# Recurrence and soft mixture of experts on one core: ScalarE evicts y ahead of VectorE, and the bonus products, the outer products, the row exponentials and one r*k product change their places in the written order

## The chip, the cores and the metric

The kernel runs on one core of a Trainium2 chip. Its engines are TensorE (PE, with its weight loads PEld), VectorE (DVE), ScalarE (ACT), GpSimd (POOL) and SyncE (SP), which issues all the DMAs. The metric is the device time of one execution in microseconds (us).

## The reference

Two parts follow each other. The first is a recurrence over 768 steps with a decaying state, for 4 batches of 8 heads of 48 channels:

```python
for t in range(S):                      # S = 768, B = 4, H = 8, D = 48
    cur = einsum('bhd,bhe->bhde', u[None] * kt, vt)          # the bonus u
    y[:, :, t] = einsum('bhd,bhde->bhe', rt, state + cur)
    state = wt[:, :, :, None] * state + einsum('bhd,bhe->bhde', kt, vt)
```

The second takes y as x (3072 rows of 384) through a soft mixture of 8 experts with 4 slots each:

```python
logits = x @ phi                                     # 3072 x 32
d = softmax over the rows;   slot_input = d.T @ x    # 32 x 384
slot_out[e] = relu(slot_input[e] @ w1[e]) @ w2[e]    # 384 -> 1024 -> 384
c = softmax over the 32 columns;   out = c @ slot_out
```

## The kernel before

**Staging.** A loop `for n in range(NIT + 1)` (L711, NIT = 16) makes one pair of heads in each iteration; `b, j = divmod(n, 4)` are its batch and its place in the batch. The 768 steps are cut into 6 chunks of 128. In what follows, "j=2" is an iteration with that j. After the loop (L839 on) come the last softmax over the rows, the experts (`up_proj`, `up_relu`, `turn`, `down_proj`) and the mixing of their outputs (`mix`).

**Order.** Nothing is scheduled by a planner: `tc.manual_schedule()` (L434) leaves every engine its instructions in the order in which they are written, and only the semaphores between the engines are put in for it, from the tiles that are read and written. So the order of the lines in the loop is the order of each engine's queue.

**The steps of iteration n** (m = n - 1 and l = n - 2 are earlier pairs whose later steps run in the same iteration), with the engine and the line under which the profile lists them:

- `b_pat(n)`: ACT L541. `b_kn(n)`: five transposes of k on PE (L548), four of them into the PSUM bank `tp1` and the fifth into `kn4`, a part of the bank `tp0`; then two copies on ACT, L550 out of `tp1` and L552 out of `kn4`.
- `c_inter(m)` (PE L615, 40 matmuls) and `c_av(m)` (PE L624, 48 matmuls) make y of the pair before in two banks `yb[0]`, `yb[1]` of one PSUM tile `y`; `c_evac(m)` adds the bonus term `avs` and writes `x`: DVE L635 for the first head, ACT L637 (a copy) and POOL L638 (the addition) for the second.
- `b_u(n)`: the outer products of k and v into `U`, in the bank `tp0` (PE L581). `b_state(n)`: a scan over them (DVE L590, `Traw`). `b_tc(n)`: ACT L597.
- `b_scores(n, hf)`: scores of one half of the chunks into the two banks of `ap` (PE L559, 12 matmuls). `b_at(n, hf)`: their eviction (ACT L564) and mask (POOL L566). Both halves use the same banks, so the second scores wait for the first eviction.
- `b_bonus(n)`: 24 small matmuls of r*k with u into `aP`, in the bank `tp0` too (PE L573), for j < 3 alone. `b_a(n)`: their copy (ACT L587). `b_av(n)`: POOL L602/L604 and L606.
- The preparation of later units u of r, k and the decays w: `a_rk` (POOL L512, r*k), `a_back` (DVE L517 scan, L520; POOL L521), `a_k` (DVE L525), `a_fwd` (DVE L528 scan), `a_r` (DVE L534), `a_chk` (POOL L537). `a_k(u)` overwrites the k that `a_rk(u)` reads.
- The softmaxes of the batch before: `l_turn(l, ypp)` turns finished x through the two banks of `y` (PE L73, ACT L650) at the end of an iteration; `l_mm` (PE L77), `s_max` (DVE L87, L88), `s_turns` (PE L109, L111; ACT L113, L115), `s_mm` (PE L120) lie between the two halves of the scores. `s_rows_exp` (DVE L145, POOL L146, ACT L147) ends the iterations with j=0 of b=2 and b=3, `s_norm` (DVE L151 to L153, POOL L154) those with j=1.

`keep_warm` (PE L674) issues matmuls on zeros. In the tail, `up_relu` evicts one half of the experts' hidden values, 512 columns, in two parts, DVE L203 and ACT L204.

Of the kernel before, what the change touches and what calls it, by code (L numbers as in the profile page):

```python
# [22 lines left out]
C = S // P  # L23
# [26 lines left out]
def rwkv_soft_moe(ctx: ExitStack, tc: tile.TileContext, wc, krc, vc, cst, w1, w2, out):  # L50
# [91 lines left out]
    def s_rows_exp(q, eng=nc.vector):  # L142
        ce = q["ce"]
        q["rm"] = rm = small.tile([P, 2 * NTG, 1], F32, name="rm")
        nc.vector.tensor_reduce(out=rm, in_=ce, axis=AX.X, op=ALU.max)  # L145
        eng.tensor_tensor(out=ce, in0=ce, in1=rm.broadcast_to([P, 2 * NTG, NS]), op=ALU.subtract)  # L146
        nc.scalar.activation(out=ce, in_=ce, func=AF.Exp)  # L147

    def s_norm(b, q, eng=nc.vector):
        ce, rm = q["ce"], q["rm"]  # L150
# [49 lines left out]

    def up_relu(h_sb, hp, hf):
        lo = 512 * hf
        nc.vector.tensor_scalar(h_sb[:, lo:lo + 256], hp[:, 0:256], 0.0, None, op0=ALU.max)  # L203
        nc.scalar.activation(out=h_sb[:, lo + 256:lo + 512], in_=hp[:, 256:512], func=AF.Relu)  # L204

    def turn(h_sb, hT, f4, tps):
        for n in range(2):
# [299 lines left out]
    def a_rk(u, k=None, c0=0, cn_=C):  # L507
        t = kr4[u % 4]
        k = t[:, 0:ROW] if k is None else k
        k3 = k.rearrange("p (c e) -> p c e", e=PIT)[:, c0:c0 + cn_, 1:PIT]  # L510
        r3 = t[:, RO:KRW].rearrange("p (c e) -> p c e", e=PIT)[:, c0:c0 + cn_, 0:P]
        nc.gpsimd.tensor_tensor(out=rks[u % 2][:, c0:c0 + cn_], in0=k3, in1=r3, op=ALU.mult)  # L512
# [31 lines left out]
    def b_kn(n):  # L544
        kt = Kt(n)
        for c in range(C - 1):
            o = tp[1][:, c * PITCH:(c + 1) * PITCH] if c < 4 else kn4
            nc.tensor.transpose(out=o, in_=kt[0:PITCH, c * PIT + 1:c * PIT + PIT], identity=ident[0:PITCH, 0:PITCH])  # L548
        src = bass.AP(tensor=tp[1].tensor, offset=tp[1].offset, ap=[tp[1].ap[0], [64, 2], [PITCH, 4], [1, D]])
        nc.scalar.copy(out=kns[n % 2][:, :, 0:4], in_=src)  # L550
        src = bass.AP(tensor=kn4.tensor, offset=kn4.offset, ap=[kn4.ap[0], [64, 2], [1, D]])
        nc.scalar.copy(out=kns[n % 2][:, :, 4], in_=src)  # L552
# [10 lines left out]
    def b_at(n, hf):  # L563
        nc.scalar.copy(out=ats[n % 2][hf].rearrange("p h c t -> p h (c t)"), in_=app[:, :, 0:384])  # L564
        at = ats[n % 2][hf].rearrange("p h c t -> p (h c) t")
        nc.gpsimd.affine_select(out=at, in_=at, pattern=[[0, 6], [1, P]], compare_op=ALU.is_gt,  # L566
                                fill=0.0, base=0, channel_multiplier=-1)

    def b_bonus(n):
        b, g = divmod(n, NG)  # L570
        for c in range(C if g < NU else 0):
            for p in range(0, P, 64):
                nc.tensor.matmul(out=aP[p:p + 64, c, :], lhsT=rks[(NU * b + g) % 2][:, c, p:p + 64],  # L573
                                 rhs=ub[:, g, :], start=True, stop=True)

    def b_u(n):
        kn, vt = kns[n % 2], vts[n % 3]
        first = [True, True]
        for c in range(C - 1):
            for h in range(2):  # L580
                nc.tensor.matmul(out=U[64 * h:64 * h + D, :, c + 1], lhsT=kn[:, h, c, :], rhs=vt[:, c, h, :],  # L581
                                 start=first[h], stop=(c == C - 2))
                first[h] = False

    def b_a(n):
        if n % NG < NU:
            nc.scalar.copy(out=asb[n % 2], in_=aP)  # L587

    def b_state(n):
        nc.vector.tensor_tensor_scan(  # L590
            out=Traw[0:PITCH].rearrange("p e n -> p (e n)"),
            data0=U[0:PITCH].rearrange("p e n -> p (e n)"),
            data1=pats[n % 2][0:PITCH].rearrange("p e n -> p (e n)"),
            initial=0.0, op0=ALU.add, op1=ALU.mult)
# [33 lines left out]
    def c_evac(n, last=False):  # L628
        b, g = divmod(n, NG)
        x = xb[b % 2]  # L630
        for h in range(2):
            xh = x[:, :, (2 * g + h) * D:(2 * g + h + 1) * D]
            yh = yb[h][:, 0:C * D].rearrange("p (c d) -> p c d", d=D)
            if h == 0 or last:
                nc.vector.tensor_tensor(out=xh, in0=yh, in1=avs[n % 2][:, h], op=ALU.add)  # L635
            else:
                nc.scalar.copy(out=xh, in_=yh)  # L637
                nc.gpsimd.tensor_tensor(out=xh, in0=xh, in1=avs[n % 2][:, h], op=ALU.add)  # L638

    def l_turn(n, pp, split=False):  # L640
        b, g = divmod(n, NG)
# [69 lines left out]
    for n in range(NIT + 1):  # L711
        b, j = divmod(n, NG)
        live = n < NIT
        m, l = n - 1, n - 2
        lb, lj = divmod(l, NG)
        sb_ = b - 1
        soft = live and 0 <= sb_ < B - 1

        u_next = NU * (b + 1) + j - 1
        if n == 0:  # L720
            a_load_w(2)
            a_load_kr(2)
        if j == 1 and live:
            a_gather(NU * b)
        if j in (1, 2) and live:
            a_gather(NU * b + j)
        if j >= 1 and u_next < B * NU and live:
            a_load_w(u_next)
            a_load_kr(u_next)
        if n + 1 < NIT:  # L730
            v_load(n + 1)
        if live:
            for _ in range(PIECES[n]):
                weight_piece()

        u0 = NU * b
        nxt = b + 1 < B
        if live:
            b_pat(n)
            if n == 0:  # L740
                a_rk(1)
                a_back(1)
            elif j == 0:
                a_fwd(u0 + 1)
                a_r(u0 + 1)
                a_chk(u0 + 1)
            elif j == 1:
                a_k(u0 + 2)
                a_fwd(u0 + 2)
            elif j == 2 and nxt:  # L750
                a_back(u0 + 3)
            elif j == 3 and nxt:
                a_r(u0 + 3)
                a_chk(u0 + 3)
                a_back(u0 + 4)
        if n == NIT:
            q = qs[b - 2]
            sp0 = tp[0][0:TG, 0:DM]
            s_mm(xb[b % 2], q, sp0)
            l_turn(l, app)  # L760
            l_mm(0, xTs[0], lpv, True, False)
            s_acc(b - 2, q, sp0)
            s_sum(b - 2, q)
            s_rows_exp(q)
            s_norm(b - 2, q)

        if live:
            b_kn(n)
        if m >= 0:
            c_inter(m)  # L770
            c_av(m)
            c_evac(m, n == NIT)
        if live:
            b_u(n)
            if n == 0:
                keep_warm(4, ap[0])
            b_scores(n, 0)
            b_at(n, 0)
            b_state(n)
        if j == 0 and b > 1 and live:  # L780
            q = qs[b - 2]
            s_mm(xb[b % 2], q, spv)
            s_acc(b - 2, q, spv)
            s_sum(b - 2, q)
        if soft and j == 1:
            l_mm(0, xTs[0], lpv, True, False)
            l_mm(1, xTs[1], lpv, False, True)
            nc.scalar.copy(out=lt_t, in_=lpv)
        if soft and j == 2:
            l_mm(2, xTs[0], lpv, True, True)  # L790
            nc.vector.tensor_tensor(out=lt_t, in0=lt_t, in1=lpv, op=ALU.add)
            qs[sb_] = q = s_max(sb_, lt_t)
        if soft and j == 3:
            s_turns(qs[sb_], dpv, lnv)
        if live:
            b_bonus(n)

        if live:
            if n == 0:
                a_k(1)  # L800
                a_fwd(1)
                a_r(1)
                a_chk(1)
            if j == 0:
                a_rk(u0 + 2)
                a_back(u0 + 2)
            elif j == 1:
                if nxt:
                    a_rk(u0 + 3)
                a_r(u0 + 2)  # L810
                a_chk(u0 + 2)
            elif j == 2 and nxt:
                a_k(u0 + 3)
                a_fwd(u0 + 3)
            elif j == 3 and nxt:
                a_rk(u0 + 4)
                a_k(u0 + 4)
        if live:
            b_a(n)
            b_tc(n)  # L820
            b_av(n)
        if live:
            if n == 0:
                keep_warm(4, ap[0])
            b_scores(n, 1)
            b_at(n, 1)
            if n == 0:
                keep_warm(8, yb[0])
        if l >= 0 and lj >= 1 and live:
            l_turn(l, ypp)  # L830
        if soft and j == 2:
            s_exp(sb_, q)
        if j == 0 and 1 < b and live:
            s_rows_exp(qs[b - 2], nc.gpsimd)
        if j == 1 and 1 < b:
            s_norm(b - 2, qs[b - 2], nc.gpsimd)


# [179 lines left out]
```

## Time and profile before

| what | value |
|---|---|
| time of the kernel, median of 3 runs (lowest to highest) | 215.06 us (213.92 to 216.74) |
| the profiled execution: its own time, its span | 215.24 us, 213.5 us |
| busy: PE, PEld, DVE, ACT, POOL | 178.5, 135.5, 111.6, 84.5, 88.1 us |
| chain that ended last: PE, DVE, POOL, ACT, DMA, issue | 54%, 14%, 10%, 7%, 6%, 5% of the span |
| mean granted TensorE clock over the span | 0.92 |
| ACT x L637 waiting for DVE x L635 | 36.6 us in 13 waits |

How to read it: the profile is one execution. The timeline gives start and duration in us from the start of the span, engine, line, operation, tiles (out<-in), shapes and the count of merged instructions; a bracket tells the idle time of the engine ahead of it and what ended that. "Windows" give, for a stretch of time, each engine's busy time with the count of its instructions in brackets, then the granted clock of TensorE (1.00 is full speed), the share of the DMA engines and GB/s. "Waits" give total us, times and the longest.

### The profile page before, as it was taken

To read this page: it belongs to the slowest core of one execution; us is meant where nothing else is said; L and a number is where in the kernel's file an instruction comes from. 1 tells how busy PE (TensorE), PEld (TensorE's weight loads), DVE (VectorE), ACT (ScalarE), POOL (GpSimd) and SP (SyncE) were. 2 spreads that over 40 slices of the span, in tenths; PEclk is the share of its full clock that TensorE was granted. 3 is DMA by queue.
4 is the path that set the end of the run, shared out by engine and by line. 5 is a ranking of instruction groups with operands and counts; after the bars stand their busy time and mean duration, and the time that the engine had idled before them with its cause. 6 is when DMAs were issued, how large, how long until landed. Compare 5 with 4: busy or idle time off the path is not lost.

```text
span 213.5 us, 7814 instructions
## 1 busy us (share of the span) xinstructions
PE 178.5 (84%) x3397; PEld 135.5 (63%) x3400; DVE 111.6 (52%) x183; ACT 84.5 (40%) x187; POOL 88.1 (41%) x130
## 2 busy tenths in 40 slices
PE   7887699977899987998988888998997977898840
PEld 2455589866797876776867766887643223776630
DVE  5886752949534594697485886142433231015330
ACT  3323051672508447355566454666512111103230
POOL 4343473685617539384665584664600000000000
PEclk9999655999559996999999999999999999999995
DMA  5995568399956849996949982699486099005682
GB/s 156 379 315 115 225 154 360 104 390 290 308 201 183 331 113 329 354 312 205 328 167 359 394 202 109 150 410 413 154 300 276 11 358 392 8 3 205 259 356 86
DMA packets 15065, 52.11 MB, mean 244 GB/s; under 512 B 1968, under 2 KB 2736, under 8 KB 15024
## 3 DMA queue, kind: packets, MB, share of 16 engines
q1 hardware_dynamic: 15024, 51.55, 69.2%
q8 instruction: 28, 0.46, 0.9%
q14 instruction: 13, 0.11, 0.1%
HBM read 44.44 MB, written 4.72 MB: 230 GB/s over the span
## 4 chain that ended last, share of the span: by engine, by line
PE 54%; DVE 14%; POOL 10%; ACT 7%; DMA 6%; issue 5%; SPq 1%; ACTq 0%; DVEq 0%; POOLq 0%
PE ap L559 10%; PE y L624 9%; DMA krb<-in_krc_dram 6%; PE G L196 5%; PE y L232 5%; DVE G L517 4%; PE y L615 4%; PE tp L581 3%; PE tp L77 3%; POOL blkat L566 3%; POOL av L606 3%; POOL blka L512 3%; PE tp L573 3%; ACT blkat L564 2%; DVE G L528 2%
## 5 line engine op out<-in xcount | busy, mean ns | idle before, releaser
L624 PE MATMUL y<-v,blkat 128*64 128x48 f32 x768 | 30.0, 238 | 4.1 <-POOL blkat L566 3.7
L564 ACT COPY blkat<-ap 128x768 f32<-128x768 f32 x32 | 25.6, 800 | 19.0 <-PE ap L559 17.7
L566 POOL TENSOR_SCALAR_AFFINE_SELECT blkat<-blkat 128x768 f32<-128x768 f32 x32 | 27.6, 863 | 8.3 <-ACT blkat L564 8.2
L624 PEld LDWEIGHTS y<-v,blkat 128*64 128x64 f32 x768 | 27.2, 151 | 5.7 <-POOL blkat L566 4.2
L559 PE MATMUL ap<-krb 48*128 48x128 f32 x288 | 25.8, 315 | 1.1 <-issue 1.0
L638 POOL TENSOR_TENSOR x<-x,av 128x288 f32<-128x288 f32 x15 | 12.0, 801 | 29.7 <-ACT x L637 29.7
L635 DVE TENSOR_TENSOR x<-y,av 128x288 f32<-128x288 f32 x17 | 7.7, 456 | 29.9 <-PE y L624 29.9
L559 PEld LDWEIGHTS ap<-krb 48*128 48x128 f32 x288 | 20.7, 210 | 3.1 <-issue 2.0
L517 DVE TENSOR_TENSOR_SCAN G<-blkw,G 128x774 f32<-128x774 f32 (+1 forms) x13 | 21.4, 1643 | 1.6 <-DMA blkw<-in_wc_dram 1.3
L528 DVE TENSOR_TENSOR_SCAN G<-blkw,G 128x774 f32<-128x774 f32 (+1 forms) x13 | 21.5, 1650 | 0.5
L637 ACT COPY x<-y 128x288 f32<-128x288 f32 x15 | 6.0, 400 | 36.6 <-DVE x L635 36.6
L512 POOL TENSOR_TENSOR blka<-krb 128x768 f32<-128x768 f32 x11 | 17.1, 1553 | 4.0 <-DMA krb<-in_krc_dram 3.2
L525 DVE TENSOR_TENSOR krb<-krb,G 128x774 f32<-128x774 f32 (+1 forms) x13 | 11.6, 891 | 12.6 <-POOL blka L512 12.6
L573 PEld LDWEIGHTS tp<-cst,blka 128*64 128x64 f32 x288 | 10.2, 145 | 6.8 <-issue 5.0
L606 POOL TENSOR_TENSOR av<-v,asb 128x576 f32<-128x576 f32 x12 | 14.1, 1177 | 0.0
L590 DVE TENSOR_TENSOR_SCAN Traw<-tp,blkm 112x288 f32<-112x288 f32 x16 | 12.0, 751 | 3.3 <-PE tp L581 3.3
L581 PE MATMUL tp<-v,blkm 128*48 128x48 f32 x320 | 11.2, 222 | 2.6 <-ACT blkm L552 2.6
L573 PE MATMUL tp<-cst,blka 128*64 128x4 f32 x288 | 11.2, 205 | 2.4 <-DVE Traw L590 1.4
L232 PE MATMUL y<-wa,x 128*32 128x160 f32 (+1 forms) x144 | 12.2, 275 | 0.7 <-issue 0.7
L615 PE MATMUL y<-Tc,krb 48*64 48x48 f32 x480 | 10.6, 236 | 2.4 <-ACT blkm L650 2.4
L196 PE MATMUL G<-wa,siT 128*32 128x512 f32 x96 | 11.3, 597 | 1.4 <-ACT x L204 1.1
L615 PEld LDWEIGHTS y<-Tc,krb 48*64 48x64 f32 x480 | 9.1, 148 | 4.8 <-ACT blkm L650 3.8
(152 smaller groups left out, 328.6 us busy)
## 6 DMA issues: line engine op xcount, KB each, us to landing
wa<-in_w_dram SPq DMA_DIRECT2D x24, 512.0 KB, 7.9
krb<-in_krc_dram SPq DMA_DIRECT2D x11, 774.5 KB, 6.4
v<-in_vc_dram SPq DMA_DIRECT2D x16, 288.0 KB, 6.1
blkw<-in_wc_dram SPq DMA_DIRECT2D x11, 387.0 KB, 3.6
wa<-in_w_dram SPq DMA_DIRECT2D x6, 640.0 KB, 5.6
out_dram<-wa SPq DMA_DIRECT2D x4, 960.0 KB, 4.4
krb<-in_w_dram SPq DMA_DIRECT2D x4, 640.0 KB, 8.4
blka<-krb SPq DMA_DIRECT2D x24, 96.8 KB, 4.7
```

What stands on the lines that cost most here:

```text
L196: nc.tensor.matmul(out=hp[32 * g:32 * g + NS, :], lhsT=siT[:, e * KT + kt, :], rhs=wts[e][:, kt * F + hf * 512:kt * F + hf * 512 + 512], s ...
L232: nc.tensor.matmul(out=so[32 * g:32 * g + NS, :], lhsT=hT[ft // 2][:, ft % 2, e, :], rhs=wts[E + e][:, FT * lo + ft * wd:FT * lo + (ft + 1 ...
L512: nc.gpsimd.tensor_tensor(out=rks[u % 2][:, c0:c0 + cn_], in0=k3, in1=r3, op=ALU.mult)
L517: nc.vector.tensor_tensor_scan(out=G[:, lo:hi][:, ::-1], data0=w[:, lo:hi][:, ::-1], data1=g_one.broadcast_to([P, hi - lo]), initial=1.0, ...
L528: nc.vector.tensor_tensor_scan(out=G[:, lo:hi], data0=ws[u % 2][:, lo:hi], data1=g_zero.broadcast_to([P, hi - lo]), initial=1.0, op0=ALU.m ...
L559: nc.tensor.matmul(out=ap[h][:, cc * P:(cc + 1) * P], lhsT=kt[64 * h:64 * h + D, c * PIT + 1:c * PIT + PIT], rhs=rt[64 * h:64 * h + D, c * ...
L564: nc.scalar.copy(out=ats[n % 2][hf].rearrange("p h c t -> p h (c t)"), in_=app[:, :, 0:384])
L566: nc.gpsimd.affine_select(out=at, in_=at, pattern=[[0, 6], [1, P]], compare_op=ALU.is_gt, fill=0.0, base=0, channel_multiplier=-1)
L573: nc.tensor.matmul(out=aP[p:p + 64, c, :], lhsT=rks[(NU * b + g) % 2][:, c, p:p + 64], rhs=ub[:, g, :], start=True, stop=True)
L606: nc.gpsimd.tensor_tensor(out=avs[n % 2], in0=vts[n % 3].rearrange("p c h d -> p h c d"), in1=a.rearrange("p c (h o) -> p h c o", o=1).bro ...
L615: nc.tensor.matmul(out=yb[h][p:p + 64, c * D:(c + 1) * D], lhsT=rt[64 * h:64 * h + D, c * PIT + p:c * PIT + p + 64], rhs=T[64 * h:64 * h + ...
L624: nc.tensor.matmul(out=yb[h][p:p + 64, c * D:(c + 1) * D], lhsT=ats[n % 2][c // 3][:, h, c % 3, p:p + 64], rhs=vt[:, c, h, :], start=False ...
```

## The change

In the loop, `b_bonus(n)` and `b_a(n)` go up to stand right behind `b_kn(n)`, ahead of `c_inter(m)`; `b_u(n)` goes down behind `b_scores(n, 0)` and `b_at(n, 0)`; `a_rk(2)`, which belongs to n = 0, goes to the end of that iteration. In `c_evac` the second head's copy on ACT and addition on POOL are written ahead of the first head's addition on DVE. `s_rows_exp` in its GpSimd form no longer issues the exponential; the loop issues it one iteration later, ahead of `s_norm`. `up_relu` evicts all 512 columns on ACT.

```diff
@@ s_rows_exp
-        nc.scalar.activation(out=ce, in_=ce, func=AF.Exp)
+        if eng is nc.vector:
+            nc.scalar.activation(out=ce, in_=ce, func=AF.Exp)
@@ up_relu
-        nc.vector.tensor_scalar(h_sb[:, lo:lo + 256], hp[:, 0:256], 0.0, None, op0=ALU.max)
-        nc.scalar.activation(out=h_sb[:, lo + 256:lo + 512], in_=hp[:, 256:512], func=AF.Relu)
+        nc.scalar.activation(out=h_sb[:, lo:lo + 512], in_=hp, func=AF.Relu)
@@ c_evac
-        for h in range(2):
-            xh = x[:, :, (2 * g + h) * D:(2 * g + h + 1) * D]
-            yh = yb[h][:, 0:C * D].rearrange("p (c d) -> p c d", d=D)
-            if h == 0 or last:
-                nc.vector.tensor_tensor(out=xh, in0=yh, in1=avs[n % 2][:, h], op=ALU.add)
-            else:
-                nc.scalar.copy(out=xh, in_=yh)
-                nc.gpsimd.tensor_tensor(out=xh, in0=xh, in1=avs[n % 2][:, h], op=ALU.add)
+        xh = [x[:, :, (2 * g + h) * D:(2 * g + h + 1) * D] for h in range(2)]
+        yh = [yb[h][:, 0:C * D].rearrange("p (c d) -> p c d", d=D) for h in range(2)]
+        if not last:
+            nc.scalar.copy(out=xh[1], in_=yh[1])
+            nc.gpsimd.tensor_tensor(out=xh[1], in0=xh[1], in1=avs[n % 2][:, 1], op=ALU.add)
+        for h in range(2 if last else 1):
+            nc.vector.tensor_tensor(out=xh[h], in0=yh[h], in1=avs[n % 2][:, h], op=ALU.add)
@@ the loop
         if live:
             b_kn(n)
+            b_bonus(n)
+            b_a(n)
         if m >= 0:
             c_inter(m)
             c_av(m)
             c_evac(m, n == NIT)
         if live:
-            b_u(n)
             if n == 0:
                 keep_warm(4, ap[0])
             b_scores(n, 0)
             b_at(n, 0)
+            b_u(n)
             b_state(n)
...
-        if live:
-            b_bonus(n)
...
             if j == 0:
-                a_rk(u0 + 2)
+                if n:
+                    a_rk(u0 + 2)
                 a_back(u0 + 2)
...
         if live:
-            b_a(n)
             b_tc(n)
             b_av(n)
...
             if n == 0:
+                a_rk(2)
                 keep_warm(8, yb[0])
...
         if j == 1 and 1 < b:
+            ce = qs[b - 2]["ce"]
+            nc.scalar.activation(out=ce, in_=ce, func=AF.Exp)
             s_norm(b - 2, qs[b - 2], nc.gpsimd)
```

## The prediction

> **What bounds the kernel now.** I read the page's chain and clock rows first, then the timeline of one iteration, then the waits, then windows.
>
> ```profile
> PEclk9999655999559996999999999999999999999995
> PE 54%; DVE 14%; POOL 10%; ACT 7%; DMA 6%; issue 5%; SPq 1%; ACTq 0%; DVEq 0%; POOLq 0%
> ```
>
> PE carries 54% of the chain that ended last, so the loop is a PE queue with holes, and an edit counts by what it does to the holes. The second reading is the clock: slices of 213.5/40 = 5.34 us, with half clock near the start (655) and twice inside the loop (55, 6).
>
> This is how one bonus iteration begins (n=10, j=2):
>
> ```profile
> 100.28 0.94 PE L559 MATMUL ap<-krb 48*128 48x128 f32 x12
> 101.15 0.87 PE L73 MATMUL y<-cst,x 128*128 128x128 f32 x6
> 101.32 0.80 ACT L564 COPY blkat<-ap 128x768 f32<-128x768 f32 x1 [0.21 <-PE ap L559]
> 101.86 0.65 PE L548 MATMUL tp<-cst,krb 112*128 112x112 f32 x5
> 102.12 0.80 ACT L650 COPY blkm<-y 128x768 f32<-128x768 f32 x1
> 102.81 0.62 ACT L541 COPY blkm<-krb 128x240 f32<-128x240 f32 x1
> 102.97 0.80 PE L615 MATMUL y<-Tc,krb 48*64 48x48 f32 x40 [0.46 <-ACT blkm L650]
> 103.34 0.48 ACT L550 COPY blkm<-tp 128x384 f32<-128x384 f32 x1
> 103.71 0.25 ACT L552 COPY blkm<-tp 128x96 f32<-128x96 f32 x1
> ```
>
> The second scores of the pair before end at 101.22. PE then turns x and keys (until 102.51) and waits 0.46 us until ACT has evicted the turned x (L650). The key copies L550 and L552 end only at 103.96, and today they run beside `c_inter` (L615): nothing on PE needs them until `b_u`.
>
> **Part 1: the bonus behind the turn of keys.** Its 24 matmuls go from between the two scores to between L548 and L615; their own time, 24 × 11.2/288 = 0.93 by the group's row, only moves. What changes is what they wait for.
>
> ```profile
> L573 PE MATMUL tp<-cst,blka 128*64 128x4 f32 x288 | 11.2, 205 | 2.4 <-DVE Traw L590 1.4 <-issue 1.0
> PE tp L573 <- DVE Traw L590: 1.4, 2, 0.7
> DVE blkm L648 <- ACT blkm L647: 1.9, 1, 1.9
> ```
>
> The bonus writes `aP` and the scan L590 reads `U`, other columns of the same PSUM bank `tp0`; yet the bonus waits for the scan. I read this as a bank being handed over whole. `kn4`, which L552 copies, lies in this bank too; behind the turn of keys the bonus must therefore wait for L552, and everything on PE, L615 and `c_av` first, is queued behind it. In n=10 the bonus could start at 103.96 + 0.05 = 104.0, where L615 starts at 102.97: **+1.0 us**. (0.05 is the step from the end of L650 to L615). L541, L550 and L552 stand in this order on ACT in every iteration, so I take 1.0 for each bonus iteration outside the start, n = 2, 4, 5, 6, 8, 9, 10, 12, 13, 14: **+10**. The bounds: 0 if the bonus need not wait, and 1.5 each, the whole hole from 102.51 to 104.0, if the present 0.46 is hidden elsewhere. ACT's own queue doesn't suffer: L587 moves ahead of ACT x L637, which waits for PE in any case.
>
> **Part 2: outer products behind the first scores.** The second scores need the first eviction: 0.05 + 0.80 + 0.05 = 0.9 us behind the first scores. Up to now the bonus filled that; now `b_u` does, with the softmax work:
>
> ```profile
> 97.04 0.66 PE L581 MATMUL tp<-v,blkm 128*48 128x48 f32 x20 [0.99 <-ACT blkm L552]
> L77 PE MATMUL tp<-blkm,cst 128*32 128x256 f32 x72 | 7.0, 388 | 0.1
> 114.20 0.39 PE L109 MATMUL tp<-cst,dT 96*128 96x96 f32 x2
> ```
>
> 0.66 plus 6 × 7.0/72 = 0.58 (j=2), twice that (j=1) or 0.39 and more (j=3) covers 0.9. Without softmax work (n=2, n=4) 0.3 stays open: +0.6, against the bonus's wait of up to 0.7 for the scan, which goes. Sum **0**. The scan comes about 0.9 later, which decides in part 3.
>
> **Part 3: ScalarE ahead of VectorE.**
>
> ```profile
> 105.45 0.46 DVE L635 TENSOR_TENSOR x<-y,av 128x288 f32<-128x288 f32 x1 [2.97 <-PE y L624]
> 105.94 0.40 ACT L637 COPY x<-y 128x288 f32<-128x288 f32 x1 [1.98 <-DVE x L635]
> ```
>
> The two readers of the tile `y` follow each other though they read different banks and write different columns, as L648 behind L647 above. The order is turned round, so ACT, and POOL behind it, come 0.49 earlier and DVE's addition about 0.43 later; `y` is free at the same time. Queued behind the addition on DVE is the scan L590, which now waits for the later `b_u` in any case. Where DVE is late the order matters (n=11, j=3):
>
> ```profile
> 114.10 0.45 DVE L635 TENSOR_TENSOR x<-y,av 128x288 f32<-128x288 f32 x1
> 114.88 0.81 ACT L564 COPY blkat<-ap 128x768 f32<-128x768 f32 x1
> 115.73 0.94 PE L559 MATMUL ap<-blka 48*128 48x128 f32 x12 [0.98 <-ACT blkat L564]
> 115.99 0.65 ACT L597 COPY Tc<-Traw 112x240 f32<-112x240 f32 x1
> 116.78 0.80 ACT L564 COPY blkat<-ap 128x768 f32<-128x768 f32 x1
> ```
>
> The first scores of n=11 ended by 114.20, where L109 follows; L564 came 0.6 late because ACT stood behind DVE, and PE lost 0.98. That stall goes. But L635, on DVE, comes at the same time as now, the scan behind it, L597 behind the scan, and the second L564 is queued behind L597. So what is late next is L597, and of 0.98 only some 0.5 reaches the next iteration: for n = 3, 7 and 11 **-1.5** (0 to -3; n=15 prepares nothing on DVE).
>
> **Part 4: exponential one iteration later.**
>
> ```profile
> 95.60 0.36 ACT L147 ACTIVATE ce<-ce 128x192 f32<-128x192 f32 x1 [2.12 <-POOL ce L146]
> ACT ce L147 <- POOL ce L146: 4.1, 2, 2.1
> ```
>
> Twice ACT stands 2 us for POOL's subtraction L146. L541 to L552 are queued behind L147, and PE waited 0.99 for L552 (the row of 97.04). That goes: 2 × -0.99. But in its new place L147 stands between L650 and L541 of n=10 and n=14, in the very row that the bonus now waits for: 2 × +0.36. Sum **-1.3**. DVE's L151 now waits for ACT at the end of j=1; queued behind it are a scan and L635 of n=10, ahead of which DVE idled 2.97 us (the row of 105.45), more than L151 can lose (the L564, L650 and L147 ahead of it on ACT come to 1.96).
>
> **Part 5: r*k of unit 2 at the end of n=0.**
>
> ```profile
> 19.39 0.20 DVE L520 RECIPROCAL blkw<-G 128x6 f32<-128x6 f32 x1
> 19.67 1.55 POOL L512 TENSOR_TENSOR blka<-krb 128x768 f32<-128x768 f32 x1 [1.87 <-DMA krb<-in_krc_dram]
> 21.16 0.19 POOL L521 COPY chk<-blkw 128x6 f32<-128x6 f32 x1
> 21.25 0.96 DVE L525 TENSOR_TENSOR krb<-krb,G 128x774 f32<-128x774 f32 x1 [1.66 <-POOL blka L512]
> 23.48 0.78 PE L624 MATMUL y<-v,blkat 128*64 128x48 f32 x10 [3.48 <-POOL blkat L566]
> ```
>
> POOL waits for a DMA, multiplies for 1.55 us, and only then gets to L521 and the mask that PE awaits for 3.48 us. Without L512 ahead of it L521 starts when L520 is done, at 19.59 instead of 21.16: PE goes on 1.57 earlier. But `a_k(2)` (L525) may overwrite k only behind L512, which now follows the mask. PE started 23.48 - 21.16 = 2.32 behind L521, so the mask ends near 19.59 + 2.27 = 21.9 and L512 near 23.4 instead of 21.2: the forward scan and L635 of the next pair, queued behind L525, come 2.2 later. I take half of the first, **-0.7** (from -1.6 to +0.6). No step that moves issues a DMA; SP's queue keeps its order.
>
> **Part 6: the relu.**
>
> ```profile
> 174.74 0.42 DVE L203 TENSOR_SCALAR x<-G 128x256 f32<-128x256 f32 x1 [2.27 <-PE G L196]
> 175.25 0.38 ACT L204 ACTIVATE x<-G 128x256 f32<-128x256 f32 x1 [1.98 <-DVE x L203]
> ```
>
> The two halves take 175.63 - 174.74 = 0.89 one behind the other. ACT copies 768 columns in 0.80 and 384 in 0.48 (L564, L550), so 512 in about 0.59: **-0.3** for the first of two; behind the second I expect PE to be busy with the next layer (0 to -0.6).
>
> **The clock.** I cut windows so that the granted clock is constant in each:
>
> ```profile
> 19.59:23.00 3.41, 0.41 (x15) 0.28 (x10) 1.72 (x2) 0.00 (x0) 3.33 (x5) 1.00 0.97 313
> 50.31:53.72 3.41, 2.12 (x39) 1.71 (x39) 3.32 (x5) 1.74 (x4) 2.23 (x4) 1.00 0.87 197
> 53.72:57.14 3.42, 3.06 (x17) 2.84 (x18) 2.26 (x2) 0.97 (x3) 3.16 (x5) 0.50 0.87 283
> 77.62:81.03 3.41, 1.58 (x28) 1.22 (x22) 2.84 (x4) 1.16 (x3) 0.86 (x3) 1.00 0.77 232
> 81.03:84.44 3.41, 3.41 (x21) 3.19 (x22) 0.87 (x1) 1.88 (x5) 3.41 (x4) 0.50 0.98 331
> 115.16:118.57 3.41, 2.37 (x31) 2.04 (x35) 0.33 (x2) 3.27 (x7) 3.41 (x4) 1.00 0.98 386
> 57.87 1.32 PE L615 MATMUL y<-Tc,krb 48*64 48x48 f32 x40
> ```
>
> A window of 3.41 us in which PE was busy for 2.12 us or less was followed by half clock (1.58 and 2.12); one with 2.37 was not (the digits from 85 us to the end of the loop are all 9). At half clock L615 takes 1.32 instead of 0.80, so a window loses 3.41 × (1 - 0.80/1.32) = 1.4 us. The loop now has four such windows (three from 53.72, digits 55; one at 81.03). Afterwards each bonus iteration has a hole of 1.5 us ahead of the bonus. It falls whole into one window with a chance of (3.41 - 1.5)/3.41 = 0.56, and then PE is busy for 1.9 at most: 10 × 0.56 = 5.6 windows. I take five for the present four: **+1.4** (from -5.6 with none to +8.4 with ten).
>
> **The sum.** 10 + 0 - 1.5 - 1.3 - 0.7 - 0.3 = +6.2, with the clock +7.6. On the profiled execution's 215.24 us (span 213.5) that is **222.8**. Its time lies 0.18 above the median of the three runs, which I let stand. 2% of 215.06 is 4.3 us, about what a measurement of this kernel can tell from no change: faster is below 210.8, slower above 219.4.
>
> **The rivals.**
>
> 1. *The bonus doesn't wait for L552.* Faster. Then part 1 is 0, and with no new hole I give back two of the four slow windows: 215.24 - 3.8 - 2.8 = **208.6**. It decides where the bonus's first matmul starts before L552 ends. Against it stands the wait for the scan, in another part of the bank; for it, that no row shows a bonus waiting for L552. The Trainium skill, "PSUM — Partial Sum Buffer", "PSUM bank collisions raise a hardware error", says to guard PSUM by bank and not by address; no run here shows what happens without.
> 2. *The start stays at full clock.* By the digits 655 the start has some 14 us of half clock, four windows, 5.6 us. It decides whether PE gets past about 2.2 us in 19.59:23.00, where it has 0.41. From part 5 it begins 1.57 earlier (1.1 us more in this window), and the bonus of n=1 adds its 0.9: it comes to 2.4 at best. Then 222.8 - 5.6 = **217.2**, no change.
> 3. *Every hole turns the clock down.* The holes are joined to the waits for L564 and the turned x, so that all ten bonus iterations pay: 215.24 + 6.2 + 8.4 = **229.8**. For it: 2.37 in 115.16:118.57 is near the limit already, and lies just where a hole of 1.0 is added.
> 4. *No hole turns the clock down,* in neither kernel: 215.24 + 6.2 - 5.6 = **215.8**, no change. It would need holes of 3.4 us. The row of 50.31 speaks against it: 2.12 us of work, half clock behind it. The Trainium skill has this rule in "TensorE: Matmul & The Clock Gate", "HAM oscillation — how this bites in real kernels": the abstract rule is "no PE-idle gaps >~3.4µs." The trace contradicts it with 1.3 us of idleness in 3.41.
>
> **How the numbers follow.** Forecast 0.52, rivals 0.13, 0.13, 0.15 and 0.07 in their order. The low end, 213, takes in rivals 4 and 2 and leaves out rival 1; the high end, 229, takes in part 1's upper bound (10 × 0.5 more, 227.8) and leaves out half of rival 3: about 0.2 outside. Faster 0.13 (rival 1). Slower 0.15 + 0.47 = 0.62, no change 0.13 + 0.07 + 0.05 = 0.25, with 0.05 of the forecast's spread below 219.4.
>
> **What would show it.** Right: L573 starts within 0.1 us of the end of L552 and PE idles 1 us or more ahead of it; L615 stands right behind L573; the idle time of L637 behind L635 is gone and L635 waits for L637 instead; L597 still comes behind a late L635 with j=3; L147 no longer waits for POOL; the mask of n=0 comes some 1.5 us earlier and L525 later; more halves in the clock row. Wrong: a bonus that starts before L552; PE's chain with as few holes as now; a start without half clock.

## The result, and the profile after

The changed kernel takes 253.13 us (median; 250.76 to 257.94) against 214.49 us (212.10 to 216.74) for the kernel before on the same chip: a ratio of 1.181, with an interval of 1.163 to 1.199. It is slower, as forecast, but by 38.6 us instead of 7.6. The profiled execution took 250.76 us. Executions of one kernel spread by several per cent with the length of their half clock (e4 below took 213.37 to 229.29 us; why was not found out), so sizes are medians of all executions, a ratio with an interval compares the faster executions of the two kernels, and mechanisms are read from the profiled execution. These are rows of its page: span, busy times, granted clock in 40 slices (now of 6.2 us), chain.

```profile
span 249.1 us, 7815 instructions
PE 211.6 (85%) x3400; PEld 160.1 (64%) x3400; DVE 110.2 (44%) x181; ACT 86.2 (35%) x187; POOL 88.4 (35%) x130
PEclk9999955555759996776659759965559999999995
PE 67%; DVE 12%; issue 7%; ACT 6%; POOL 4%; DMA 2%; SPq 0%; ACTq 0%; POOLq 0%; DVEq 0%
```

The span grew by 249.1 - 213.5 = 35.6 us, and PE's busy time by 211.6 - 178.5 = 33.1 us, for the same matmuls. So PE stood idle only 2.5 us longer. The clock row says why: it is full of fives. The mean granted clock fell from 0.922 to 0.788, which at two levels, full and half, makes 2 × 0.212 × 249.1 = 105.6 us of half clock against 2 × 0.078 × 213.5 = 33.3 us: 72 us more, or 21 windows of 3.41 us. At the prediction's 1.4 us each these are 29.4 us, most of the loss. In the loop the half clock comes in seven stretches, 99.0 us or 29 windows in all; before it came in three, 27.3 us or 8 windows.

PE's waits (total, times, longest, in us) show the hole that was forecast:

```profile
PE tp L573 <- ACT blkm L552: 16.0, 11, 2.4
PE tp L573 <- POOL av L606: 2.1, 1, 2.1
PE y L624 <- POOL blkat L566: 1.3, 1, 1.3
PE tp L548 <- DVE Traw L590: 1.1, 1, 1.1
```

The list of before had these:

```profile
PE ap L559 <- ACT blkat L564: 4.4, 5, 1.8
PE y L615 <- ACT blkm L650: 3.6, 8, 0.6
PE tp L581 <- ACT blkm L552: 2.6, 3, 1.0
```

The waits of L615 for the turned x and of L581 for L552 are gone; the wait of L559 for L564 is down to one of 0.4. One iteration (n=10) in the timeline:

```profile
118.29 0.37 ACT L837 ACTIVATE ce<-ce 128x192 f32<-128x192 f32 x1
118.55 0.59 ACT L541 COPY blkm<-krb 128x240 f32<-128x240 f32 x1
119.41 0.25 ACT L552 COPY blkm<-tp 128x96 f32<-128x96 f32 x1
119.71 1.45 PE L573 MATMUL tp<-cst,blka 128*64 128x4 f32 x24 [1.73 <-ACT blkm L552]
121.09 1.21 PE L615 MATMUL y<-Tc,krb 48*64 48x48 f32 x35
```

L552 ends at 119.66 and the bonus (L573) starts 0.05 us later, after 1.73 us of idleness. But it runs for 1.45 us, not 0.9: the clock has gone down. Four windows of the clock (length, busy time of PE, PEld, DVE, ACT, POOL with counts, granted clock, DMA share, GB/s):

```profile
34.42:37.83 3.41, 3.41 (x50) 3.22 (x48) 0.46 (x1) 0.40 (x1) 0.80 (x1) 0.50 1.02 410
65.14:68.55 3.41, 2.39 (x90) 2.16 (x89) 1.55 (x1) 1.31 (x5) 1.21 (x2) 1.00 0.51 201
106.09:109.50 3.41, 2.30 (x90) 2.23 (x92) 2.97 (x4) 1.24 (x5) 2.75 (x5) 1.00 0.63 250
174.36:177.77 3.41, 3.41 (x83) 3.32 (x82) 0.00 (x0) 1.51 (x6) 0.75 (x1) 0.50 0.53 108
```

The second and third hold one hole, the bonus, L615 and half of L624; PE is busy for 2.39 and 2.30 us, and half clock follows. The first and last lie within stretches of half clock that last 34.1 us (from 31.0) and 23.9 us (from 164.1); in these two windows PE is busy all the time. The other five stretches last two or three windows. So one drop cost from two to ten windows.

### The profile page after: what moved, and what is told of

It reads as the page before. It is cut to its first block, busy times and chain, and to the rows that moved or that the text cites. A ratio compares the mean times of both kernels' runs of the same rounds, so it can differ in the third digit from the quotient of the medians.

```text
span 249.1 us, 7815 instructions
## 1 busy us (share of the span) xinstructions
PE 211.6 (85%) x3400; PEld 160.1 (64%) x3400; DVE 110.2 (44%) x181; ACT 86.2 (35%) x187; POOL 88.4 (35%) x130
## 4 chain that ended last, share of the span: by engine, by line
PE 67%; DVE 12%; issue 7%; ACT 6%; POOL 4%; DMA 2%; SPq 0%; ACTq 0%; POOLq 0%; DVEq 0%
PE y L624 12%; PE ap L559 12%; PE y L615 5%; PE G L197 4%; PE tp L581 4%; PE tp L573 4%; PE y L232 4%; PE y L73 4%; PE tp L77 3%; PE tp L120 3%; PE tp L548 3%; DVE G L528 3%; DVE G L517 3%; POOL blka L512 2%; DVE krb L534 2%
## 5 line engine op out<-in xcount | busy, mean ns | idle before, releaser
L624 PE MATMUL y<-v,blkat 128*64 128x48 f32 x768 | 36.7, 272 | 1.3 <-POOL blkat L566 1.3
L624 PEld LDWEIGHTS y<-v,blkat 128*64 128x64 f32 x768 | 34.2, 187 | 2.6 <-POOL blkat L566 1.4
L564 ACT COPY blkat<-ap 128x768 f32<-128x768 f32 x32 | 25.7, 803 | 25.8 <-PE ap L559 25.3
L566 POOL TENSOR_SCALAR_AFFINE_SELECT blkat<-blkat 128x768 f32<-128x768 f32 x32 | 27.6, 862 | 18.2 <-ACT blkat L564 18.2
L559 PE MATMUL ap<-krb 48*128 48x128 f32 x288 | 32.2, 377 | 0.4 <-ACT blkat L564 0.4
L559 PEld LDWEIGHTS ap<-krb 48*128 48x128 f32 x288 | 26.5, 267 | 8.4 <-issue 5.3
L573 PE MATMUL tp<-cst,blka 128*64 128x4 f32 x288 | 12.3, 214 | 18.1 <-ACT blkm L552 16.0
L573 PEld LDWEIGHTS tp<-cst,blka 128*64 128x64 f32 x288 | 11.4, 161 | 20.7 <-ACT blkm L552 16.7
L512 POOL TENSOR_TENSOR blka<-krb 128x768 f32<-128x768 f32 x11 | 17.1, 1550 | 2.5 <-DMA krb<-in_krc_dram 2.5
L525 DVE TENSOR_TENSOR krb<-krb,G 128x774 f32<-128x774 f32 (+1 forms) x13 | 11.5, 888 | 10.3 <-POOL blka L512 10.3
L597 ACT COPY Tc<-Traw 112x240 f32<-112x240 f32 x16 | 9.9, 619 | 12.9 <-DVE Traw L590 12.9
L581 PE MATMUL tp<-v,blkm 128*48 128x48 f32 x320 | 14.3, 257 | 0.0
L581 PEld LDWEIGHTS tp<-v,blkm 128*48 128x48 f32 x320 | 12.0, 166 | 3.0 <-issue 2.2
L615 PE MATMUL y<-Tc,krb 48*64 48x48 f32 x480 | 12.4, 258 | 0.0
```

Source lines behind the costliest of these rows:

```text
L559: nc.tensor.matmul(out=ap[h][:, cc * P:(cc + 1) * P], lhsT=kt[64 * h:64 * h + D, c * PIT + 1:c * PIT + PIT], rhs=rt[64 * h:64 * h + D, c * ...
L615: nc.tensor.matmul(out=yb[h][p:p + 64, c * D:(c + 1) * D], lhsT=rt[64 * h:64 * h + D, c * PIT + p:c * PIT + p + 64], rhs=T[64 * h:64 * h + ...
L624: nc.tensor.matmul(out=yb[h][p:p + 64, c * D:(c + 1) * D], lhsT=ats[n % 2][c // 3][:, h, c % 3, p:p + 64], rhs=vt[:, c, h, :], start=False ...
```

## The experiments

My theory after the comparison: the wait for L552 behind the shared bank is the cause, and it costs by the clock, not by idleness. The rivals: idleness and queue order themselves; one of the other edits; or a clock that looks only at how long PE is busy.

### Which edit: e1 and e2

```diff
# e1_bonus_back: the changed kernel
             b_kn(n)
-            b_bonus(n)
-            b_a(n)
...
+        if live:
+            b_bonus(n)      # behind the softmax work, as before
...
+            b_a(n)          # ahead of b_tc, as before
# e2_bonus_only: the kernel before with this move alone
```

> The changed kernel with the bonus and its copy back in their old places; all other edits stay. Theory (the bonus's wait for the copy L552 makes holes of 1.3 to 2.6 us, 16.0 us in all, and the holes drop the clock, 99 us of half clock instead of 27): the waits of L573 for L552 are gone, half clock falls to 30 us or less, the time to 207 to 216. Rival A (the other moves, above all the outer products behind the first scores, keep TensorE's work too thin for the clock): half clock stays above 60 us and the time above 230. Rival B (the late addition on VectorE costs): 220 to 230, with L590 and L597 ahead of the holes.

> The kernel before with the bonus and its copy moved behind the turn of keys and nothing else. Theory: most of the loss, 235 to 258, with 12 to 18 us of waits of L573 for L552 and 60 us of half clock or more. Rival A: within 8 us of the kernel before. Rival B: 220 to 230.

Measured: e1 217.67 us (215.64 to 235.29), the kernel before 216.96 (207.98 to 224.91) on the same chip; e2 245.52 us (242.41 to 248.59). Longest waits of PE in e2:

```profile
PE tp L573 <- ACT blkm L552: 21.7, 12, 4.7
PE ap L559 <- ACT blkat L564: 10.0, 10, 2.5
```

The move of the bonus alone costs 28.6 us; all the other edits together change nothing in the time that can be told. Without those edits the bonus move also opens holes ahead of the second scores (10.0 us against 4.4 us before), as nothing is left to fill the first eviction.

Two things don't fit the theory. In e2 half of the loss is idleness: of a span that is 28.5 us longer (242.0 us) PE is busy for 13.4 us more (191.9 us) and idle for 15.1. Only together with the other edits is the loss nearly all clock. And e1's time is 1.7 us above the range that I expected, with 61 us of half clock in the loop of its profiled execution (224.24 us) where I had 30 at the most.

### The bank: e3

```diff
-    aP = tp[0][:, D * C:D * C + 4 * C].rearrange("p (c n) -> p c n", n=4)
+    aP = ap[0][:, 384:384 + 4 * C].rearrange("p (c n) -> p c n", n=4)
```

> The changed kernel with the bonus's product in columns 384 to 407 of the first bank of the scores, which no one else uses, instead of in the bank of the fifth turned key. Everything stands where the change puts it, only the shared bank is gone. Theory: L573 follows L548 without a hole, L552 is waited for by no one on TensorE, half clock 10 to 30 us, 203 to 213. Rival A (the place of the bonus, not its bank): holes ahead of L573 or L615 as long as in the changed kernel, above 235. Rival B: 220 to 230.

Measured: 214.22 us, 1 us above the range of the theory, ratio 0.988 (0.972 to 1.003); 211.15 us in the profiled execution. The wait for L552 is gone, and what PE waits for now is

```profile
PEclk9999755556999999999996589999999999999965
PE y L624 <- POOL blkat L566: 3.7, 4, 2.1
PE ap L573 <- ACT blkat L564: 1.8, 3, 0.7
```

One line of address moves the time by some 39 us: the shared bank is the whole loss. That the bonus's columns and `kn4` don't overlap didn't help. In its new place too the bonus waits for a reader of other columns, L564 (the last row). Whether it is the bank or the tile that is handed over whole isn't separated: `tp0` is one bank and one tile, and e3 changes both. Yet the kernel is not clearly faster than before, although PE's holes are 10 us shorter in all (209.4 - 184.5 = 24.9 us of idleness against 213.5 - 178.5 = 35.0): the start has 27 us of half clock (digits 5555), twice as much as before.

### Clock or idleness: e4, e6, e8, e9

e4 leaves the bank and the wait, and fills the hole with five dummy matmuls of 128 x 128 and 512 columns; e9 is the same kernel again, beside e8, whose dummies use 32 x 32 of the array. e6 makes the hole shorter by moving L541 behind L552.

```diff
# e4_filled_hole, e9_heavy_fill; e8_light_fill has keep_light(5, ap[0])
             b_kn(n)
+            if n and j < 3:
+                keep_warm(5, ap[0])
             b_bonus(n)
# e8: out=bank[0:32, 0:512], lhsT=zb[0:32, 0:32], rhs=zb[0:32]
# e6_short_hole
-            b_pat(n)
...
             b_kn(n)
+            b_pat(n)
             b_bonus(n)
```

> The changed kernel with five matmuls on zeros (0.25 us each, no use to the result) between the turn of keys and the bonus in each iteration that has one, n = 1 and up: TensorE works through the hole, and the bonus starts no earlier. Theory (it is the clock that costs, not the waiting itself): half clock 30 us or less and 214 to 224. Rival (the waits cost as such, or zeros don't hold the clock): half clock above 70 us, 245 to 260.

> The changed kernel, shared bank and all, with one ScalarE instruction moved: the copy of the pattern (L541, 0.6 us) stands behind the two key copies instead of ahead of them, so L552 ends 0.6 us earlier and the hole ahead of the bonus shrinks from 1.45 to about 0.85 us, 16.0 to about 9.5 us in all. Theory clock: with a hole under 1 us most windows keep PE busy for more than 0.7 of them and the clock stays: half clock falls from 99 us in the loop to under 50, and the time from 253 by 6.5 us of idleness and some 14 windows at 1.4 to 220 to 232. Rival (idle time alone): 253 - 6.5 = 246 to 248.

> The changed kernel with the hole ahead of the bonus filled by five dummy matmuls as in e4_filled_hole, but each uses 32 x 32 of the array instead of 128 x 128, at the same 512 columns and the same 0.21 us: PE is as busy, with a sixteenth of the dummies' work. Theory work (what sets the clock is how much of the array the matmuls use, not how long PE is busy): the windows with the bonus, c_inter and c_av keep their small work and the clock falls as in the changed kernel, 60 us or more of half clock in the loop, 235 to 255 us. Rival busy time: the same as the heavy dummies, 213 to 229, at most 25 us of half clock in the loop.

> e4_filled_hole once more, on the same chip as the light dummies, for a direct comparison and because its four times lay far apart (213.4 to 229.3). Expected of both theories: 213 to 229, and a profile with at most 25 us of half clock in the loop.

Measured: e4 224.29 us (213.37 to 229.29), e9 225.42 (221.38 to 226.86), e8 244.45 (238.28 to 260.69), e6 239.22 (227.42 to 247.51). The clock rows, of e4 (213.37 us), of e9 (226.86 us), of e8 (243.35 us) and of e6 (247.51 us):

```profile
PEclk9999699999999999999999999999999999999955
```

```profile
PEclk9999555557999999999998559999999999999985
```

```profile
PEclk9997555566759997599755555999999999999985
18.18:21.57 3.39, 3.12 (x92) 2.37 (x90) 1.59 (x2) 0.32 (x2) 1.70 (x4) 1.00 0.76 174
```

```profile
PEclk9999955555558995699555557566799999999975
PE tp L573 <- ACT blkm L552: 11.2, 11, 1.9
```

Heavy dummies take 28 us off the changed kernel (e9 is at a ratio of 1.054, 1.014 to 1.095, to the kernel before), although the bonus starts no earlier behind L552 than without them; so the waiting is not the main cost. They don't hold the clock everywhere: half clock in the loop is 3.4 us in e4, but 44.4 us in e9, where I had expected 25 at the most, and 30.7 of these lie in one stretch at the start. Light dummies, which keep PE busy as long, leave 244 us and 88.7 us of half clock: the second row of e8 is a window in which PE was busy for 3.12 of 3.39 us, and half clock follows. The two differ in the part of the array that they use, so the time that PE is busy is not what counts by itself.

e6 is a miss for both theories in its size. By the medians the shorter hole took 14 us off, less than the theory's 21 to 33 and more than the rival's 5 to 7. The holes shrank to 11.2 us in 11 waits, yet this execution has more half clock in the loop than the changed kernel's (105.8 against 99.0 us), and holes of 0.93 us (n=13) and 1.24 us (n=10) were followed by it. So a hole of 1 us is still long enough; how the loss grows with the length isn't settled. The reading that fits e8 is that the windows behind the turned keys hold little work in any case (L573, L615 and L624 use 64 of 128 columns of the array, L615 48 rows), so that a small hole is enough; for e6 itself that is argued, not shown.

### The price of one hole: e5 and e10

e5 is e3 with dummies in the three places where it stood idle; e10 puts aP back into the shared bank for three iterations.

```diff
# e5_bank_and_fill: e3 and
-                keep_warm(8, yb[0])        # end of n=0
+                keep_warm(18, yb[0])
+            if n == 2:                     # behind b_kn
+                keep_warm(6, yb[0])
+        if j == 3 and nxt and live:        # ahead of l_turn
+            keep_warm(5, tp[1])
# e10_three_holes: e5 with tp[0]'s aP for n in (5, 9, 13)
```

> The changed kernel with aP in the other bank, and dummy matmuls in three places where PE still stood idle: 18 instead of 8 at the end of n=0 (the wait for the mask), 6 behind the turned keys of n=2, 5 ahead of the turned x of n=3, 7, 11. Theory clock (what the change loses are half-clock windows that PE's holes set off): the start from 23.05 and the stretch from 111.8 stay at full clock; e3_other_bank had 27.3 + 10.2 us of half clock in the loop, 11 windows at 1.4 us, so its 211.15 should come to 196 to 200, with the granted clock at 0.95 or more, although PE is given 21 to 39 more dummies of 0.21 us. Rival (the holes count by their idle time alone): the dummies only replace idle time, 210 to 214.

> e5_bank_and_fill (204.2 us, 6.8 us of half clock in the loop), with aP back in the shared bank for three iterations only, n = 5, 9 and 13: the price of one hole by itself. Idle time: L573 waits for L552 there, 3 times 1.0 to 1.5 us. Theory clock: each hole can turn the clock down for one to three windows of 3.41 us, 1.4 us each, so 3 to 13 us in all on top of what part of the waiting counts: 208 to 218. Rival (idle time alone): 206 to 208.5, half clock as in e5_bank_and_fill.

Measured: e5 204.22 us (202.44 to 209.91), ratio 0.958 (0.950 to 0.967): faster than the kernel before. It came out 4 us above the range that I expected; its profile still has 6.8 us of half clock in the loop. e10 takes 213.29 us (210.31 to 216.10), as the theory expected. A row of e5 and two of e10, where the lines are one further down:

```profile
PEclk9999999999999999999997599999999999999965
```

```profile
PEclk9999999999579999999999965899999999999965
PE tp L574 <- ACT blkm L553: 4.3, 3, 1.5
```

Three holes of 1.43 us cost 9 us by the medians and 5.7 by the spans of the profiled executions (208.6 and 202.9): 2 to 3 us each, where their idleness is 1.43. Two of the three set off half clock (digits 57 and 658), of two and three windows; the one between them didn't, and e5's own two windows are not there. Eleven such holes would make 21 to 33 us.

### What ends half clock: e13 and e14

The same burst of 20 dummies ahead of the bonus of n=2, inside the half clock that e3 has from 23 us on, once with 128 x 128 of the array and once with 32 x 32.

```diff
# e13_heavy_burst; e14_light_burst has keep_light(20, yb[0]); both on e3
             b_kn(n)
+            if n == 2:
+                keep_warm(20, yb[0])
             b_bonus(n)
```

> The changed kernel with aP in the other bank, and 20 dummy matmuls of 128 x 128 with 512 columns in one burst ahead of the bonus of n=2, inside the 27 us of half clock that e3_other_bank has from 23.05 us. Theory work: two windows full of such matmuls hold enough work even at half clock, and the clock returns within two windows of the burst's start (by about 36 us instead of 50); half clock at the start falls to 10 to 14 us. At half clock the burst itself takes up to 20 x 0.43 = 8.5 us, less the wait that it replaces (1 to 2 us), against some four windows won at 1.4 us: 211 to 217. Rival (half clock lasts a time of its own, or ends at the softmax matmuls of the next batch element): half clock from 23 to about 55 us, 218 to 222.

> The same burst of 20 dummies in the same place, each using 32 x 32 of the array (columns and duration the same, a sixteenth of the work). Theory work: PE is busy all the time but the windows hold little work, so the clock does not return: half clock from 23 us to 50 us or beyond, 218 to 225. Rival (a busy PE brings the clock back): as with the heavy burst, back by about 36 us, 211 to 217.

Measured: e13 211.56 us (210.97 to 212.23), e14 222.44 us (219.41 to 228.21; ratio 1.041, 1.021 to 1.062). Windows of e13, then of e14:

```profile
24.06:27.47 3.41, 3.41 (x40) 2.83 (x37) 3.35 (x4) 0.80 (x1) 2.79 (x3) 0.50 0.24 91
27.48:30.88 3.40, 3.40 (x12) 1.50 (x11) 3.21 (x4) 2.28 (x5) 2.48 (x5) 0.50 0.33 46
30.90:34.30 3.40, 3.40 (x28) 1.55 (x26) 0.00 (x0) 0.00 (x0) 0.34 (x2) 1.00 0.93 333
```

```profile
27.93:31.33 3.40, 3.38 (x10) 1.16 (x9) 2.98 (x4) 2.26 (x5) 2.33 (x6) 0.50 0.41 58
31.35:34.75 3.40, 3.40 (x9) 1.13 (x8) 0.00 (x0) 0.00 (x0) 0.11 (x1) 0.50 0.90 334
34.76:38.16 3.40, 3.40 (x26) 1.56 (x24) 0.00 (x0) 0.00 (x0) 0.00 (x0) 0.50 0.97 387
```

The heavy burst, from 28.16 us, brings the clock back at the end of the window in which it starts; the light burst, from 28.53 us, fills two windows just as fully, and half clock goes on to 58.6 us (34.1 us in all). So a busy PE doesn't end a stretch; the part of the array that the burst uses decided here.

What ends the stretches of the real work is open. I found no weighting of rows and columns that sorts all the windows, and narrowness by itself doesn't explain the long ones. In e2 eight of twelve stretches in the loop lasted one window, some with nothing but narrow matmuls in it, as this one (L615, L624 and L581), behind which full clock follows:

```profile
69.52:72.93 3.41, 3.41 (x72) 3.40 (x68) 0.46 (x1) 0.01 (x1) 0.00 (x0) 0.50 1.00 374
```

A rival that no run isolates is the place of `b_u`. In the profiles, one execution each, of the kernels that have it ahead of the first scores (before, e2, e12) no stretch in the loop is longer than 13.7 us; behind them stretches of 27 to 51 us occur (the changed kernel, e1, e3, e6, e7, e8, e9, e14), though not in all (e4, e5, e10, e11, and e13 with its burst).

### Single parts: e7, e11, e12

```diff
# e7_rk_back: e3 with r*k of unit 2 in its old place
-                if n:
-                    a_rk(u0 + 2)
+                a_rk(u0 + 2)
...
-                a_rk(2)            # end of n=0
# e11_old_evac: e5 with DVE's addition of y ahead of ACT's copy
# e12_before_filled: the kernel before, keep_warm(24, yb[0]) at the end of
#   n=0 and keep_warm(5, tp[1]) ahead of l_turn for n=3, 7, 11
```

> The changed kernel with aP in the other bank, and the third r*k back in its old place (beginning of what follows the first scores of n=0). Tests part 5 of the prediction and whether the moved multiplication is what makes the start fall to half clock. If it is: no or a shorter stretch of half clock behind 23 us, where e3_other_bank had 27.3 us of it, and a time below 207. If the start falls all the same, because PE waits for the mask of n=0 in both: half clock from 23 us on again, second half of the first c_av 0.2 to 1.5 us later, a_k(2) (L525) 2 us earlier, and a time of 209 to 217, the same as e3_other_bank within what the length of that stretch makes.

> e5_bank_and_fill with the eviction of y in its old order, VectorE ahead of ScalarE: part 3 by itself, at a clock that is mostly full. The prediction put the new order at -1.5 us (0 to -3), all of it at n = 3, 7, 11, where L564 stands behind ScalarE's copy and that behind a late VectorE. If so: 205.5 to 207.5, and PE waits for L564 ahead of the second scores of n = 7 and 11 for some 1 us each. Rival (the dummies ahead of the turned x at j=3, or VectorE's coming earlier by 0.4 us, make up for it): 203 to 205.

> The kernel before with dummy matmuls in the places of e5_bank_and_fill where it too stands idle: 24 instead of 8 at the end of n=0 (its wait for the mask is 3.48 us), 5 ahead of the turned x of n=3, 7, 11. Is what made e5_bank_and_fill faster than the kernel before (204.2 against 216.7 us) the dummies alone, or also the change with its bank moved? Theory (the change without the shared bank saves holes, 18.2 us of them in e3_other_bank against 28.3 before, and this stays when the clock is held): the dummies give the kernel before the start's four half-clock windows back, 5.6 us, and leave the holes ahead of the second scores: 207 to 212. Rival (the dummies are all of it): 202 to 206, as fast as e5_bank_and_fill.

Measured: e7 214.83 us (210.97 to 220.59), not to be told from e3; the start falls to half clock in both. e12 209.56 us, ratio 0.989 (0.980 to 0.999): the dummies alone bring some 5 us by the medians, 1% by the ratio; with the moved bank the change brings another 5 (204.22; 3% by the ratios), and PE stands idle for 23.5 us in e5 against 32.8 in e12. e11 218.05 us (216.92 to 218.64), ratio 1.030 (1.020 to 1.041) against e5's 0.958, far above both ranges that I had expected. PE's longest wait in e11, and n=11 in its timeline:

```profile
PE ap L559 <- ACT blkat L564: 12.1, 7, 3.4
113.30 0.45 DVE L634 TENSOR_TENSOR x<-y,av 128x288 f32<-128x288 f32 x1
113.79 0.40 ACT L636 COPY x<-y 128x288 f32<-128x288 f32 x1 [3.58 <-DVE x L634]
114.08 0.81 ACT L564 COPY blkat<-ap 128x768 f32<-128x768 f32 x1
114.94 0.90 PE L559 MATMUL ap<-blka 48*128 48x128 f32 x8 [2.25 <-ACT blkat L564]
```

In e5 the same wait is

```profile
PE ap L559 <- ACT blkat L564: 1.5, 4, 0.4
```

ACT stands 3.58 us for the late VectorE, the first eviction stands behind ACT's copy, and PE idles 2.25 us ahead of the second scores. The order of the eviction is worth some 14 us in e5. The profiled spans differ by 13.4 us (216.3 and 202.9), and PE's busy time by 6.3 of these (185.7 and 179.4): about half is idleness, and half is the clock, with 23.9 us of half clock in e11's loop and 6.8 in e5's.

## Why the prediction was right and wrong

- **Part 1** was right in its mechanism: the bonus starts 0.05 us behind L552 (0.14 at the start), in 11 waits of 1.45 us on average, near the upper bound of 1.5 (single ones reach 2.4, behind iterations with j=3). L837 in front of L541 lengthens it at n=10, as part 4 said. Wrong was to add +10 to the sum: the same iterations lost their waits for the turned x, for L564 and for L552 ahead of `b_u`, which I had taken only in part. All idleness together grew by 2.5 us, where my terms gave +6.2; that PE at half clock has less to wait for may be part of this.
- **Part 2** held: with nothing to fill them, the second scores of e5 wait 0.37 us for the first eviction (its row above, 1.5 us in 4; I had 0.3); the changed kernel has one such wait of 0.4.
- **Part 3** named the right mechanism, and its size of -1.5 was far too small: some 14 us with the bonus moved, in e5's surroundings (e11). My reading is that the bonus no longer covers what ACT loses behind a late VectorE; no run isolates this. The pattern that I forecast for j=3 is there (n=11):

```profile
135.52 0.42 DVE L637 TENSOR_TENSOR x<-y,av 128x288 f32<-128x288 f32 x1
136.64 0.62 ACT L597 COPY Tc<-Traw 112x240 f32<-112x240 f32 x1 [1.03 <-DVE Traw L590]
137.06 0.84 ACT L564 COPY blkat<-ap 128x768 f32<-128x768 f32 x1
139.68 0.52 PE L573 MATMUL tp<-cst,blka 128*64 128x4 f32 x12 [2.33 <-ACT blkm L552]
```

- **Part 4** held. L837 no longer waits for POOL (no bracket in its row above), and L581's wait for L552 is gone.
- **Part 5** was wrong in the gain. PE waits 1.30 us for the mask of n=0 instead of 3.48, but the mask is only 0.20 us earlier (23.28 instead of 23.48), not 1.57: PE itself came later, with `c_av` of n=0 from 21.07 instead of 19.09. Behind L520 the mask does follow sooner (L566 starts 1.66 us behind the start of L520 instead of 3.18), but L520 itself came at 20.70 instead of 19.39, which I had not reckoned with. And the delay that the move was to save belonged to the one profile of before: in e7 L512, in its old place, ran from 18.50 to 20.05, was over before L520 (20.13), and L566 follows 1.66 us behind. L525 came at 24.78 instead of 21.25, later than the 2.2 us that I took, and at n=2 the bonus now stands for POOL:

```profile
20.70 0.20 DVE L520 RECIPROCAL blkw<-G 128x6 f32<-128x6 f32 x1
23.28 0.91 PE L624 MATMUL y<-v,blkat 128*64 128x48 f32 x24 [1.30 <-POOL blkat L566]
24.78 0.96 DVE L525 TENSOR_TENSOR krb<-krb,G 128x774 f32<-128x774 f32 x1 [3.89 <-POOL blka L512]
31.01 1.45 PE L573 MATMUL tp<-cst,blka 128*64 128x4 f32 x24 [2.08 <-POOL av L606]
```

  The start's half clock came at 31.0 instead of 23.0, behind this wait, and lasted 34.1 us.
- **Part 6**: PE's one wait for the relu (L204) went from 1.1 to 0.8 us; I had -0.3.
- **The clock is the step that failed.** I took +1.4 us: five windows of half clock in the loop for four, as if each drop cost one. Measured are 21 windows more over the span: 10 instead of 4 in the stretch at the start, and 19 instead of 4 in the rest of the loop. The number of drops was about right: 5.6 holes were to turn the clock down, and six drops behind the start did, each in a window with a bonus hole. But each cost two to seven windows, and the first stretch of before in the middle of the loop, three windows at 53.73, had already shown that one drop can cost more than one. Light and heavy bursts (e14, e13) show that half clock can go on while PE is busy all the time, which the term left out. The criterion "busy for 2.12 us or less" failed too: windows with 2.39 and 2.30 us turned the clock down, and in e8 one with 3.12; that the count came out is in part luck. The price of a window, 1.4 us, was a fair size (the sum written there gives 1.3, and L559, with 1.65 instead of 0.94 us, 1.5). Rival 3 had the right sign of it, every hole pays, but at 1.4 us each; e10 shows 2 to 3, idleness included, in a kernel whose clock is otherwise held.
- **The Trainium skill**, "TensorE: Matmul & The Clock Gate", "What's actually happening", has full clock return after about one busy window of 3.4 us. The heavy burst agrees (one window, 27.48 to 30.88); the light burst speaks against it, with half clock over consecutive windows of 3.38 to 3.40 us busy. The rule of rival 4, no gaps over some 3.4 us, falls with holes of 1.0 to 1.5 us.

## What to carry to other kernels

Before an engine's work is moved, look at which PSUM bank and tile its output lies in and what reads them at the new place: moving 24 numbers per row to another bank decided 39 us here. A hole on TensorE can cost more than its idle time, as several windows at half clock may follow it, and how many wasn't predictable here. Dummy matmuls that use the whole array helped where PE stood idle anyway (28 us off the changed kernel); ones that merely keep it busy for as long helped far less (9 us).

## What the runs showed of the hardware that I had not expected

- With PE busy for 3.40 of 3.40 us, half clock persisted under 32 x 32 matmuls and ended after the one window in which 128 x 128 matmuls of the same columns began (e14, e13).
- Half clock lasted up to 51.2 us in one stretch (e7, 22.7 to 73.9 us), in which PE was busy all the time.
